# Weights decoded in pieces of twice the width, second half of x split three tiles at a time, w_out prepared two chunks at once

## The chip, the core and the metric

The kernel runs on one core of a Trainium2 chip, with its five engines: TensorE (PE, matrix products into PSUM banks), VectorE (DVE), ScalarE (ACT), GpSimd (POOL) and SyncE (SP), which here only issues DMAs. The metric is the time of one execution on the device in microseconds. Engines run their own instruction lists in order and meet through semaphores, so an instruction that waits also holds up everything behind it on its engine.

## The reference

Causal attention over 4 batches, 12 heads, 448 positions and head width 64, followed by two matrix products with a PReLU between them. The inputs q, k and v are float32. The two weights are float64 as they come.

```python
scores = scale * np.matmul(q, k.transpose(0, 1, 3, 2))
scores = np.where(mask, -1000000000.0, scores)      # causal
attn = np.exp(scores - max) / (sum + 1e-09)
x = np.matmul(attn, v)            # laid out as (1792, 768)
h = x @ w_in                      # (768, 2048)
g = np.maximum(h, 0.0) + alpha * np.minimum(h, 0.0)
out = g @ w_out                   # (2048, 768)
```

## The kernel before

**Products.** Both large products use a scheme of seven block products in place of eight (`STEPS`: P1, P5, P6, P2, P7, P3, P4). Its operands are blocks (A11, A12, A21, A22 of w_in, B11 to B22 of x or w_out) and sums of blocks (S1 to S4, T1 to T4). Each operand is split in a high part, which TensorE takes, and a low part, the rest; so every operand costs one cast on ACT (`a_cast`, `t_hi`, `w_cast`, `g_cast`) and one subtraction, called "lo" below, on DVE or POOL (`a_lo`, `t_lo`, `w_lo`, `g_lo`), beside the sums themselves (`a_sum`, `w_sum`, `g_sum`).

**Stages.** First comes attention, over 24 pairs of heads, in an order written out by hand (`ORDER`, `ROUNDS`). Into its iterations a table `EARLY` puts decoding work and splits of the first half of x (batches 0 and 1); the letters A, C, D, +, LD in it are the steps of a decode, h and l the cast and lo of one tile of x, S, cast and sub the sums and splits of w_in. Then comes the first product (line 395 on PE, `h_step`): 8 groups of 256 columns of w_in, each with 7 steps for each half of x (b = 0 and 1). Group 0 of the first half runs inside the end of attention. Groups 1 to 6 alternate b step by step; group 7 does b = 0 and then b = 1. The second product (line 1183, `o_step`) runs over four quarters Q of w_out's rows; each quarter has 7 tiles of 128 rows, taken in pairs that go on across the quarters' borders.

**Decoding.** A float64 weight arrives as two 32-bit words. `p_load` fetches a piece into a "raw" buffer (lines 273 and 278), ACT takes the magnitude of the high word (`p_abs`, line 290) and the scaled low word (`p_int`, 295), POOL or DVE clamps (`p_clamp`, 311 or 303), DVE shifts (`p_shift`, 303) and puts the sign back (`p_sign`, 319), POOL adds both words (`p_add`, 327). A piece has 384 values a partition: 32 pieces for w_in, 32 for w_out. A decoded piece of w_out is stored to DRAM (`wd`, line 331) and read back in the second product (line 1105). There are three raw buffers, two in the tile `dec` and one in `tf` that comes free after the split of T2 and T4; a raw buffer is given back after the sign.

**The order after attention** is made by a planner (`Plan`): jobs with an engine, a cost (`US`), dependencies, buffers that they take and give (`rooms`), and due times worked back from PE's list; each engine's order follows from it. It is fixed when the program is built. The handover from attention to the planned part holds the splits of the second half of x (`x2_jobs`): six operands of three tiles, 448 values a partition each, cast on ACT and subtracted on DVE or POOL (line 665). The first group's `h_plus` (line 409) on DVE, which adds a kept bank to another, stands between P6 and P7.

**w_out in the second product.** For each quarter and each of its two chunks u, `w_jobs` loads four blocks, makes four sums (line 1110) and seven splits (line 1121), all on DVE with 384 values a partition. The buffers of the quarter before come free step by step.

Of the kernel before, what the change touches and what calls it, by code (L numbers as in the profile page):

```python
# [21 lines left out]
CP = 112  # L22
QP = 128
WARM = 8
EARLY = {
# [25 lines left out]
    "abs": 0.56, "int": 0.56, "clamp": {"POOL": 0.53, "DVE": 0.48}, "shift": 0.48, "sign": 0.57, "add": 1.07, "cast": 0.53, "cast448": 0.57,  # L51
# [5 lines left out]
SHARED = {"sign", "sum", "lo", "lo448", "gsum", "glo"}  # L57
# [100 lines left out]
class Slots:  # L158
# [21 lines left out]
def kernel(  # L180
# [61 lines left out]
    def dec_of(i):  # L242
        return dec[:, 12 + i * NH : 12 + (i + 1) * NH]

    RAW = 2 * P + 2

    def rows_of(x, n):
        return x.bitcast(I32).rearrange("p (a n) -> p a n", n=n)[:, :, : 2 * P]  # L250
# [9 lines left out]
    raws, xs, ys, ss, wi = {}, {}, {}, {}, {}  # L260
# [7 lines left out]
    def p_load(key):  # L268
        kind, f, z = key
        t = raws[key] = rooms["raw"].take()  # L270
        if kind == "i":
            rows = w_in32[z * NH : (z + 1) * NH, 2 * f * P : 2 * (f + 1) * P]
# [1114 lines left out]
```

## Time and profile before

| | us |
|---|---|
| median of 3 runs | 618.72 (617.91 to 620.41) |
| the profiled execution | 618.8 |
| its span, first to last instruction | 617.0 |
| PE busy in the span | 582.4 (94%) |
| DVE busy | 506.6 (82%) |
| ACT busy | 403.0 (65%) |
| POOL busy | 314.4 (51%) |

The span lies 1.8 us below the execution's own time, and the profiled execution is 0.1 us from the median. PE is busy nearly throughout, so what can change the end is where PE waits, and at which clock it runs: the profile shows a granted clock of 1.0 (2.4 GHz) or 0.5 (1.2 GHz). A wait of PE has a releaser, the instruction that ended it, and the question at each is what stood in front of that releaser on its own engine.

### The profile page before, as it was taken

To read this page: it belongs to the slowest core of one execution; us is meant where nothing else is said; L and a number is where in the kernel's file an instruction comes from. 1 tells how busy PE (TensorE), PEld (TensorE's weight loads), DVE (VectorE), ACT (ScalarE), POOL (GpSimd) and SP (SyncE) were. 2 spreads that over 40 slices of the span, in tenths; PEclk is the share of its full clock that TensorE was granted. 3 is DMA by queue.
4 is the path that set the end of the run, shared out by engine and by line. 5 is a ranking of instruction groups with operands and counts; after the bars stand their busy time and mean duration, and the time that the engine had idled before them with its cause. 6 is when DMAs were issued, how large, how long until landed. Compare 5 with 4: busy or idle time off the path is not lost.

```text
span 617.0 us, 10794 instructions
## 1 busy us (share of the span) xinstructions
PE 582.4 (94%) x3300; PEld 502.0 (81%) x3300; DVE 506.6 (82%) x1118; ACT 403.0 (65%) x1002; POOL 314.4 (51%) x395
## 2 busy tenths in 40 slices
PE   8999999999975999999888989999999999988997
PEld 5666666667754989999777978999999999978997
DVE  5999888898479798988888795889788999887853
ACT  6999998888375665766566663778665755653521
POOL 7757687775354445554555431412635524581520
PEclk9999999999996999999899999999999999997999
DMA  6965636323053587867776737555242342221433
GB/s 166 215 130 159 171 89 185 107 75 118 17 159 123 169 252 236 292 208 248 238 236 210 253 141 240 159 163 163 81 133 70 93 132 82 82 70 55 166 90 116
DMA packets 100601, 93.98 MB, mean 152 GB/s; under 512 B 12736, under 2 KB 98848, under 8 KB 100544
## 3 DMA queue, kind: packets, MB, share of 16 engines
q1 hardware_dynamic: 99648, 91.66, 48.8%
q0 software_dynamic: 576, 1.18, 0.7%
q8 instruction: 26, 0.43, 0.3%
q10 hardware_dynamic: 320, 0.46, 0.2%
q14 instruction: 31, 0.25, 0.1%
HBM read 64.72 MB, written 28.54 MB: 151 GB/s over the span
## 4 chain that ended last, share of the span: by engine, by line
PE 77%; DVE 10%; DMA 6%; issue 3%; ACT 2%; SPq 1%; POOL 0%; ACTq 0%; DVEq 0%
PE bank L1183 27%; PE bank L395 26%; PE bank L602 7%; PE bank L582 7%; PE bank L525 6%; PE bank L517 4%; DMA dec<-in_moe_w_in_dram 2%; DVE x1h L1121 2%; DVE x2l L665 1%; DVE x1l L1161 1%; DVE dec L1110 1%; DMA tf<-gd 1%; DMA acc<-gd 1%; DMA dec<-wd 1%; SPq L1131 1%
## 5 line engine op out<-in xcount | busy, mean ns | idle before, releaser
L506 POOL TENSOR_SCALAR p<-p,rs 128x128 f32<-128x128 f32 (+3 forms) x164 | 83.8, 529 | 32.8 <-PE bank L525 11.1
L552 ACT ACTIVATE p<-bank,nm 128x256 f32<-128x256 f32 (+3 forms) x168 | 82.3, 505 | 14.8 <-DVE nm L537 9.1
L1183 PE MATMUL bank<-x1h,x1l 128*128 128x384 f32 x399 | 77.6, 336 | 2.4 <-DVE x1h L1121 1.9
L537 DVE CUSTOM_DVE_ANT_0 bank<-bank,mask 128x128 f32<-128x128 f32 (+3 forms) x168 | 71.1, 481 | 9.3 <-PE bank L525 5.4
L1183 PEld LDWEIGHTS bank<-x1h,x1l 128*128 128x128 f32 x399 | 70.0, 188 | 3.7 <-DVE x1h L1121 2.9
L1183 PE MATMUL bank<-x1h,gset 128*128 128x384 f32 x294 | 60.3, 343 | 0.9 <-DVE tf L1197 0.9
L419 ACT ACTIVATE tf<-bank 128x448 f32<-128x448 f32 x64 | 33.7, 541 | 38.1 <-PE bank L395 16.8
L1183 PEld LDWEIGHTS bank<-x1h,gset 128*128 128x128 f32 x294 | 53.2, 192 | 1.3 <-DVE tf L1197 1.3
L582 PEld LDWEIGHTS bank<-ident,p 128*128 128x128 f32 x384 | 43.3, 141 | 12.1 <-issue 8.1
L395 PE MATMUL bank<-x1h,wir 128*128 128x448 f32 x192 | 45.7, 371 | 5.6 <-DVE wir L377 5.1
L602 PEld LDWEIGHTS bank<-ptf,v 128*64 128x64 f32 x384 | 25.4, 136 | 30.8 <-issue 13.0
L395 PE MATMUL bank<-x2h,wir 128*128 128x448 f32 x174 | 43.2, 386 | 7.2 <-DVE bank L409 7.2
L423 DVE SCALAR_TENSOR_TENSOR tf<-tf,om,bank 128x448 f32<-128x448 f32 x64 | 41.8, 674 | 8.7 <-ACT tf L419 8.6
L582 PE MATMUL bank<-ident,p 128*128 128x128 f32 x384 | 47.5, 274 | 0.7 <-POOL p L506 0.5
L602 PE MATMUL bank<-ptf,v 128*64 128x448 f32 (+3 forms) x384 | 46.8, 386 | 0.0
L395 PEld LDWEIGHTS bank<-x2h,wir 128*128 128x128 f32 x174 | 35.0, 202 | 11.1 <-DVE bank L409 7.8
L395 PEld LDWEIGHTS bank<-x1h,wir 128*128 128x128 f32 x192 | 35.7, 188 | 10.1 <-DVE wir L377 6.2
L525 PE MATMUL bank<-kr,qr 64*128 64x128 f32 (+2 forms) x288 | 43.3, 404 | 0.0
L502 ACT ACTIVATE ptf<-bank 128x512 f32<-128x512 f32 (+1 forms) x71 | 38.0, 583 | 1.7 <-PE bank L582 1.7
L303 DVE TENSOR_SCALAR dec<-dec 128x384 int32<-128x384 int32 (+1 forms) x62 | 33.9, 546 | 5.8 <-POOL dec L311 3.1
L395 PE MATMUL bank<-x1h,wie 128*128 128x448 f32 x144 | 33.9, 368 | 4.4 <-DVE wie L377 4.4
L327 POOL TENSOR_TENSOR dec<-dec 128x384 int32<-128x384 int32 x26 | 28.6, 1102 | 17.9 <-DVE dec L319 10.1
(176 smaller groups left out, 1458.1 us busy)
## 6 DMA issues: line engine op xcount, KB each, us to landing
gd<-tf SPq DMA_DIRECT2D x64, 224.0 KB, 3.7
dec<-in_moe_w_in_dram SPq DMA_DIRECT2D x24, 384.0 KB, 3.9
dec<-in_moe_w_out_dram SPq DMA_DIRECT2D x22, 384.0 KB, 3.6
tf<-gd SPq DMA_DIRECT2D x28, 256.0 KB, 4.6
acc<-gd SPq DMA_DIRECT2D x28, 256.0 KB, 3.9
dec<-wd SPq DMA_DIRECT2D x28, 192.0 KB, 3.6
kr<-in_k_dram SPq DMA_DIRECT2D x44, 112.0 KB, 3.4
qr<-in_q_dram SPq DMA_DIRECT2D x47, 96.0 KB, 3.0
```

The costliest lines, as they stand in the source:

```text
L303: ts(out=out.bitcast(dtype), in0=x.bitcast(dtype), **how)
L395: nc.tensor.matmul(ps, w[:, u, k * P : (k + 1) * P], x[:, k], start=(st in ("P1", "P5") and i == 0), stop=(i == len(mms) - 1), skip_group_ ...
L419: nc.scalar.activation(t, bank_of(g, b, role), AF.Relu, scale=-1.0)
L423: stt(out=t, in0=t, scalar=om[:, f : f + 1], in1=bank_of(g, b, role), op0=ALU.mult, op1=ALU.add)
L502: eng.activation(out, x, AF.Copy, scale=side)
L506: eng.tensor_scalar(out=out, in0=x, scalar1=side, scalar2=1.0, op0=ALU.mult, op1=ALU.mult)
L525: nc.tensor.matmul(ps[:, o : o + lim], T["q", p][half(j), i * QP : (i + 1) * QP], T["k", p][half(j), :lim], start=(o == 0), stop=(n > 0 or ...
L537: nc.vector.tensor_tensor_reduce(out=t, in0=t, in1=masks[1] if i == NQ else masks[0][:, (NQ - 1 - i) * QP :], scale=-SCALE, scalar=MOST_F3 ...
L552: nc.scalar.activation(T["p", p, i][:, j, : t.shape[1]], t, AF.Exp, scale=-1.0, bias=T.pop(("nm", p, i, j)), accum_out=T["sm", p][:, z : z ...
L582: nc.tensor.transpose(ps[:, j - js[0], c], t[:, j, c * QP : (c + 1) * QP], T["ident"])
L602: nc.tensor.matmul(out[half(j), c * QP :], vs[b % 2][:, hp, c, j], x[:, c * QP : S], start=(c == 0), stop=(c == NQ),)
L1183: nc.tensor.matmul(ps, x, w, start=(st in ("P1", "P5")[: 1 if Q else 2] and i == 0), stop=(i == len(mms) - 1), skip_group_check=True,)
```

## The change

Four things change together.

1. A piece of the decode has 768 values a partition in place of 384: 16 pieces for w_in (both column halves of a group at once) and 16 for w_out (a whole chunk). The magnitude, clamp, shift and sign now work in place on the buffer `y`; the scaled low word is left in the raw buffer, which is therefore given back only after the add. There are two raw buffers of twice the size (one in `dec`, one in `tf`) in place of three, and four buffers y of twice the size in place of nine and three x. In attention three pieces are decoded early in place of five half-size ones.
2. The second half of x is cast and subtracted as a whole operand, 1344 values at once, except T1, which keeps its three tiles; all subtractions are on DVE, none on POOL. The loads of B21 and B22 are one DMA each.
3. The blocks of w_out are loaded, summed, cast and subtracted for both chunks of a quarter at once, 768 values, and sums T2, T3 and T4 overwrite one of their inputs.
4. The last three pieces of w_out (`LATE`) are loaded after the first product's last step and decoded in the first quarter of the second product, in space that later holds sums of output tiles 4 to 6.

The costs in `US` follow the new widths. The core of the diff:

```diff
+LATE = 3
...
-    25: "cast:A12 cast:S3 sub:A12 sub:S3", 26: "cast:S4 cast:A22 sub:S4 sub:A22",
+    25: "cast:A12 cast:S3 sub:A12 sub:S3", 26: "D:2 cast:S4 cast:A22 D:2 sub:S4 sub:A22 +:2:0 +:2:1 LD",
...
-        "raw": Slots([rows_of(dec[:, 3 * RAW * i : 3 * RAW * (i + 1)], RAW) for i in range(2)]),
-        "y": Slots([dec_of(i) for i in range(4, 8)]), "x": Slots([dec_of(i) for i in range(8, 10)]),
+        "raw": Slots([raw_of(dec_of(0, 4))]), "y": Slots([dec_of(i, 2) for i in (4, 6, 8)]),
...
+        low = parts_of(key)[0]
+        nc.scalar.activation(low.bitcast(I32), low, AF.Copy, scale=2.0**-29)
+
+    def p_clamp(key, eng=nc.gpsimd):
+        y = ys[key]
+        eng.tensor_scalar(out=y, in0=y, scalar1=MOST, scalar2=LEAST, op0=ALU.min, op1=ALU.max)
 
     def p_shift(key):
-        p_move(key, I32, scalar1=3, scalar2=0x3FFFFFF8, op0=ALU.logical_shift_left, op1=ALU.bitwise_and)
+        y = ys[key].bitcast(I32)
+        ts(out=y, in0=y, scalar1=3, scalar2=0x3FFFFFF8, op0=ALU.logical_shift_left, op1=ALU.bitwise_and)
...
+        y = line(ys[key]).bitcast(I32)
+        stt(out=y, in0=parts_of(key)[1], scalar=-0x40000000, in1=y, op0=ALU.bitwise_and, op1=ALU.bitwise_or)
+
+    def p_add(key, part=None):
+        y, low = line(ys[key]).bitcast(I32), parts_of(key)[0].bitcast(I32)
+        if part is not None:
+            y, low = y[:, :, part * P : part * P + P], low[:, :, part * P : part * P + P]
+        nc.gpsimd.tensor_tensor(out=y, in0=y, in1=low, op=ALU.add)
+        if part != 0:
+            rooms[room_of(key, "raw")].give(raws.pop(key))
...
+                for p in parts(nm):
+                    def hi(nm=nm, p=p):
+                        nc.scalar.activation(flat_of(XH[1][nm], nm, p), flat_of(x32(nm), nm, p), AF.Copy)
+
+                    def lo(nm=nm, p=p):
+                        x, h, l = (flat_of(t, nm, p) for t in (x32(nm), XH[1][nm], XL[1][nm]))
+                        nc.vector.tensor_tensor(out=l, in0=x, in1=h, op=ALU.subtract)
+
+                    n = S * (p[1] - p[0])
+                    job(("xh", nm, p), "ACT", f"cast{n}", hi, of)
+                    job(("x", 1, nm, p), "DVE", f"lo{n}", lo, [("xh", nm, p)])
...
+        at_end = T0 + (NG - 1) * PER
+        for j, key in enumerate(late_keys):
+            piece_jobs(key, before, at_end + 8.0 * j + 20.0, [("P", NG - 1, 1, "P4")])
+            before = key
...
+        def w_sum(Q, nm):
+            x, y = (at[Q, b] for b in W_SUMS[nm])
+            if nm == "T1":
+                t = at[Q, nm] = rooms["ws"].take()
+            else:
+                t = at[Q, nm] = at.pop((Q, {"T2": "T1", "T3": "B12", "T4": "B21"}[nm]))
+            nc.vector.tensor_tensor(out=t, in0=x, in1=y, op=ALU.subtract)
...
+            T1, T2 = (("wsum", Q, b) for b in ("T1", "T2"))
+            made = {
+                "B11": [B11], "T1": [B12, B11], "T2": [B22, T1, ("wlo", Q, "T1")], "B21": [B21], "T3": [B22, T1], "B22": [B22],
+                "T4": [T2, ("wlo", Q, "B21")],
...
+                        if t > 3:
+                            pl.wait_issue(pl.named[kind, q], [("store", key) for key in late_keys])
```

On DVE at the handover, before: from the last attention sum (L621) to the first group's two bank additions (L409) and the first activations (L423). The x2l rows are the lo parts of the second half of x, dec rows with L303 and L319 are shift and sign.

```order
L621 TENSOR_TENSOR tf<-bank_65,tf 128x448
L303 TENSOR_SCALAR dec<-dec 128x3x128
L319 SCALAR_TENSOR_TENSOR dec<-dec 128x384
L303 TENSOR_SCALAR dec<-dec 128x3x128
L319 SCALAR_TENSOR_TENSOR dec<-dec 128x384
L665 TENSOR_TENSOR x2l<-tf,x2h 128x448 x5
L303 TENSOR_SCALAR dec<-dec 128x3x128
L319 SCALAR_TENSOR_TENSOR dec<-dec 128x384
L665 TENSOR_TENSOR x2l<-x2l,x2h 128x448 x2
L665 TENSOR_TENSOR x2l<-tf,x2h 128x448 x3
L665 TENSOR_TENSOR x2l<-x2l,x2h 128x448 x2
L409 TENSOR_TENSOR bank_65<-bank_64,tf 128x448
```

On DVE at the same place now (L620, L961, L408, L307 and L311 are the same operations).

```order
L620 TENSOR_TENSOR tf<-bank_65,tf 128x448
L961 TENSOR_TENSOR x2l<-tf,x2h 128x448 x3
L961 TENSOR_TENSOR x2l<-tf,x2h 128x1344 x2
L961 TENSOR_TENSOR x2l<-x2l,x2h 128x1344
L408 TENSOR_TENSOR bank_65<-bank_64,tf 128x448
L961 TENSOR_TENSOR x2l<-x2l,x2h 128x1344
L307 TENSOR_SCALAR dec<-dec 128x768
L961 TENSOR_TENSOR x2l<-tf,x2h 128x1344
L311 SCALAR_TENSOR_TENSOR dec<-dec 128x768
L408 TENSOR_TENSOR bank_61<-bank_64,tf 128x448
```

The first bank addition stood behind twelve tiles of x and six steps of decode; now it stands behind T1's three tiles and three whole operands, and no decode step.

On SP in the middle of the first product, before: loads of pieces (L273, L278), stores of decoded w_out (L331) and of results (L429).

```order
L273 DMA dec<-in_moe_w_in_dram 128x3x256
L429 DMA gd_85<-tf 128x448 x2
L331 DMA wd<-tf 128x384
L278 DMA dec<-in_moe_w_out_dram 128x3x256
L429 DMA gd_85<-tf 128x448
L331 DMA wd<-tf 128x384
L273 DMA tf<-in_moe_w_in_dram 128x3x256
L278 DMA dec<-in_moe_w_out_dram 128x3x256
L273 DMA dec<-in_moe_w_in_dram 128x3x256
```

On SP in the middle of the first product now (L277 and L282 are the loads, L322 the stores of w_out, L428 of results).

```order
L277 DMA dec<-in_moe_w_in_dram 128x3x512
L428 DMA gd_85<-tf 128x448 x2
L322 DMA wd<-dec 128x768
L277 DMA tf<-in_moe_w_in_dram 128x3x512
L282 DMA dec<-in_moe_w_out_dram 128x1536
L428 DMA gd_85<-tf 128x448 x2
L282 DMA tf<-in_moe_w_out_dram 128x1536
L428 DMA gd_85<-tf 128x448 x3
L322 DMA wd<-dec 128x768
L277 DMA dec<-in_moe_w_in_dram 128x3x512
```

The loads now go to the two tiles in turn, one buffer each, where two of three went to `dec`; each brings twice as much.

On DVE where the fourth quarter begins, before: the rows between the additions of tiles 20 and 21 (L1197 from bank_67 and bank_68), of which tile 21 is the first of the fourth quarter; L1110 are sums and L1121 lo parts of its w_out.

```order
L1197 TENSOR_TENSOR bank_64<-bank_68,acc 128x384
L1110 TENSOR_TENSOR dec<-dec 128x384
L1197 TENSOR_TENSOR acc<-bank_65,acc 128x384 x2
L1197 TENSOR_TENSOR bank_63<-bank_67,tf 128x384
L1121 TENSOR_TENSOR x1h<-dec,x1h 128x384 x2
L1110 TENSOR_TENSOR dec<-dec 128x384
L1121 TENSOR_TENSOR x1l<-dec,x1l 128x384
L1121 TENSOR_TENSOR wie<-dec,wie 128x384
L1121 TENSOR_TENSOR x1h<-dec,x1h 128x384
L1110 TENSOR_TENSOR dec<-dec 128x384
L1110 TENSOR_TENSOR dec<-x1l,dec 128x384
L1197 TENSOR_TENSOR bank_61<-bank_68,acc 128x384
```

On DVE at the same place now (L1241 are the additions, L1165 the lo parts, L1206 a split of g).

```order
L1241 TENSOR_TENSOR bank_64<-bank_68,acc 128x384
L1165 TENSOR_TENSOR x1h<-dec,x1h 128x2x384
L1206 TENSOR_TENSOR x1l<-acc,x1l 128x512
L1241 TENSOR_TENSOR acc<-bank_65,acc 128x384
L1241 TENSOR_TENSOR bank_63<-bank_67,tf 128x384
L1241 TENSOR_TENSOR acc<-bank_65,acc 128x384
L1241 TENSOR_TENSOR bank_61<-bank_68,acc 128x384
```

Between tile 21's two bank additions stood eight instructions on w_out; now there is one, and four of the quarter's seven operands are split before tile 20 begins.

## Rows read from the trace of the kernel before

**Rows 1.** The page: its head.
```profile
span 617.0 us, 10794 instructions
```

**Rows 2.** Busy time by stretch: stretch, us, busy us of each engine (instructions), granted clock, DMA.
```profile
164.40:201.00 36.60, 25.65 (x110) 20.25 (x110) 26.50 (x35) 20.39 (x45) 17.28 (x17) 0.86 0.36 119
201.00:395.20 194.20, 183.83 (x884) 166.23 (x883) 165.28 (x302) 121.40 (x254) 89.76 (x97) 0.99 0.68 222
395.20:614.00 218.80, 210.33 (x1177) 207.17 (x1175) 176.33 (x274) 122.09 (x250) 89.99 (x62) 0.98 0.37 110
```

**Rows 3.** Waits of PE: engine, line, releaser, us in total, times, longest.
```profile
PE bank L395 <- DVE bank L409: 7.7, 3, 6.8
PE bank L395 <- DVE wir L377: 5.1, 3, 2.3
PE bank L1183 <- DVE wie L1121: 4.5, 2, 4.3
PE bank L395 <- DVE wie L377: 4.4, 2, 2.5
```

**Rows 4.** Timeline at the handover, of PE, DVE, ACT: start, us, instructions, idle before.
```profile
174.50 2.92 ACT L502 ACTIVATE x2h<-tf 128x448 fp32r<-128x448 f32 x6 [0.65 <-DMA xd_B<-low_B]
...
175.58 5.19 DVE L665 TENSOR_TENSOR x2l<-tf,x2h 128x448 fp32r<-128x448 f32 x5
...
192.22 0.62 DVE L409 TENSOR_TENSOR bank<-bank,tf 128x448 f32<-128x448 f32 x1
...
192.89 2.61 PE L395 MATMUL bank<-x2h,wir 128*128 128x448 f32 x6 [6.80 <-DVE bank L409]
...
200.91 1.39 PE L395 MATMUL bank<-x1h,wie 128*128 128x448 f32 x6
...
204.59 1.39 PE L395 MATMUL bank<-x1h,wir 128*128 128x448 f32 x6
```

**Rows 5.** Loads of pieces, 203 to 356 us: first, last, and grouped with landing time.
```profile
203.35 0.38 SPq L278 DMA_DIRECT2D dec<-in_moe_w_out_dram  x1
...
355.07 0.38 SPq L278 DMA_DIRECT2D dec<-in_moe_w_out_dram  x1
...
dec<-in_moe_w_out_dram SPq DMA_DIRECT2D x21, 384.0 KB, 3.6
dec<-in_moe_w_in_dram SPq DMA_DIRECT2D x14, 384.0 KB, 3.7
tf<-in_moe_w_out_dram SPq DMA_DIRECT2D x10, 384.0 KB, 4.0
...
tf<-in_moe_w_in_dram SPq DMA_DIRECT2D x7, 384.0 KB, 4.4
```

**Rows 6.** DMA issues of the whole run: KB each, median us to landing.
```profile
b<-xd_B SPq DMA_DIRECT2D x1, 672.0 KB, 4.9
```

**Rows 7.** Groups by shape: count, busy us, mean ns; L303's row: shortest, median, longest ns.
```profile
L377 DVE TENSOR_TENSOR wie<-dec,wie 128x384 fp32r<-128x384 f32 x16 | 8.8, 553 | 0.3 <-ACT wie L374 0.3
L1161 DVE TENSOR_TENSOR x1l<-dec,x1l 128x512 fp32r<-128x512 f32 x11 | 7.5, 682 | 0.2 <-ACT x1l L1157 0.2
L303 DVE TENSOR_SCALAR tf<-tf x21: 352/690/1169, 204.6 to 356.0; 128x384 int32<-128x384 int32 x18, 128x384 f32<-128x384 f32 x3
L327 POOL TENSOR_TENSOR tf<-tf,dec 128x384 int32<-128x384 int32 x20 | 20.3, 1017 | 21.8 <-DVE dec L319 15.6 <-ACT wir L374 2.6 <-ACT dec L290 2.1
L374 ACT ACTIVATE wir<-dec 128x384 fp32r<-128x384 f32 x25 | 12.8, 524 | 3.8 <-DVE dec L345 2.9 <-POOL dec L327 0.8
L1157 ACT ACTIVATE x1l<-dec 128x512 fp32r<-128x512 f32 x19 | 11.9, 627 | 8.7 <-DVE dec L1151 8.1 <-POOL dec L1151 0.4
```

**Rows 8.** Timeline where the fourth quarter begins, of DVE and PE.
```profile
551.99 2.53 DVE L1121 TENSOR_TENSOR x1h<-dec,x1h 128x384 fp32r<-128x384 f32 x2
554.45 1.61 DVE L1110 TENSOR_TENSOR dec<-dec 128x384 f32<-128x384 f32 x1
...
558.12 1.01 PE L1183 MATMUL bank<-wie,x1l 128*128 128x384 f32 x2 [4.30 <-DVE wie L1121]
```

More of the change, by code (lines that the diff above doesn't have):

```diff
@@ L50 @@
 US = {
-    "abs": 0.56, "int": 0.56, "clamp": {"POOL": 0.53, "DVE": 0.48}, "shift": 0.48, "sign": 0.57, "add": 1.07, "cast": 0.53, "cast448": 0.57,
+    "abs": 0.82, "int": 0.82, "clamp": {"POOL": 0.83, "DVE": 0.56}, "shift": 0.56, "sign": 0.97, "add": 2.02, "cast": 0.53,
+    "cast448": 0.57, "cast1344": 1.2, "lo1344": 1.55, "wsum": 0.95, "wcast": 0.8, "wlo": 0.95,
     "sum": {"DVE": 0.57, "POOL": 1.15}, "lo": {"DVE": 0.56, "POOL": 1.15}, "lo448": {"DVE": 0.63, "POOL": 1.25},
@@ L55 @@
 }
-SHARED = {"sign", "sum", "lo", "lo448", "gsum", "glo"}
+SHARED = {"clamp", "shift", "sign", "sum", "lo", "lo448", "lo1344", "gsum", "glo", "wsum", "wlo"}
 LOAD, STORE = 4.0, 3.0
@@ L268, in p_load @@
     def p_load(key):
[L269 to L272, printed above, removed]
+        t = raws[key] = rooms[room_of(key, "raw")].take()
+        if key[0] == "i":
+            _, g, z = key
+            rows = w_in32[z * NH : (z + 1) * NH, 4 * g * P : 4 * (g + 1) * P]
             nc.sync.dma_start(
@@ L323, in p_sign @@
-        rooms["raw"].give(raws.pop(key))
-    def p_add(key):
-        y, x = ys[key].bitcast(I32), xs[key].bitcast(I32)
-        nc.gpsimd.tensor_tensor(out=y, in0=y, in1=x, op=ALU.add)
-        rooms["x"].give(xs.pop(key))
+        y = line(ys[key]).bitcast(I32)
[7 more added lines that the diff above has]
+            rooms[room_of(key, "raw")].give(raws.pop(key))
@@ L966, in x_of @@
                 return []
-            return [("x", 1, nm, k) for k in range(KW)]
+            return [] if nm == "B11" else [("x", 1, nm, p) for p in parts(nm)]
         def step_job(g, b, st):
@@ L1187, in o_step @@
             if t == NTT - 1:
-                for u in range(2):
-                    rooms["w"].give(wo.pop((Q, u, bn)).rearrange("p u n -> p (u n)"))
+                rooms["w"].give(wo.pop((Q, bn)).rearrange("p u h n -> p (u h n)"))
             if q % 2:
@@ new lines, in w_jobs @@
+            for c, z in ((0, 0), (0, 1), (1, 1), (1, 0)):
+                job(
+                    ("wl", Q, f"B{c + 1}{z + 1}"), "SP", "issue", lambda c=c, z=z: w_load(Q, c, z),
+                    dec_end + [("store", ("o", 4 * Q + c + 2 * u)) for u in range(2)], "wf", lag=LOAD, behind=list(wl_last),
+                )
+                wl_last[:] = [("wl", Q, f"B{c + 1}{z + 1}")]
+            B11, B12, B22, B21 = (("wl", Q, b) for b in ("B11", "B12", "B22", "B21"))
+            T1, T2 = (("wsum", Q, b) for b in ("T1", "T2"))
@@ new lines, in w_jobs, with give @@
+            made = {
+                "B11": [B11], "T1": [B12, B11], "T2": [B22, T1, ("wlo", Q, "T1")], "B21": [B21], "T3": [B22, T1], "B22": [B22],
+                "T4": [T2, ("wlo", Q, "B21")],
+            }
+            gives = {"B11": "B11", "T1": "B11", "T2": "B22", "T3": "B22", "T4": "T2"}
+            def give(nm):
+                n = W_READS.get(nm, 1)
+                return [("ws" if nm == "T2" else "wf", Q, nm, n)]
+            for st in STEPS:
+                nm = STEP[st][1]
+                of = made[nm]
+                if nm[0] == "T":
+                    job(("wsum", Q, nm), "DVE", "wsum", lambda nm=nm: w_sum(Q, nm), of, "ws" if nm == "T1" else "", give(gives[nm]))
+                    of = [("wsum", Q, nm)]
+                job(("wcast", Q, nm), "ACT", "wcast", lambda nm=nm: w_cast(Q, nm), of, "w")
+                job(
+                    ("wlo", Q, nm), "DVE", "wlo", lambda nm=nm: w_lo(Q, nm), [("wcast", Q, nm)],
+                    give=[] if nm in ("T1", "B21") else give(nm),
+                )
```

294 lines of the change are left out of this document (133 added, 161 removed), and 6 rows, old and new, of the table EARLY.

## The prediction

> **What bounds the kernel now.** I read the page's head [rows 1], then busy time by stretch [rows 2], then the waits of PE with their releasers [rows 3], then the timelines around the two longest of them [rows 4, 8], and last the loads and the groups by shape [rows 5 to 7]. The stretches show PE busy 184 of 194 us in the first product and 210 of 219 in the second; only the handover is loose, 25.7 of 36.6, with a granted clock of 0.86 [rows 2]. So the end is PE's own work plus three sets of waits. One is the wait of 6.8 us on L409 at the handover, followed by matmuls at the half clock: 2.61 us for six at 192.89, where six take 1.39 at 200.91 [rows 3, 4]. The second is the first product's waits for weights, 5.1 + 4.4 = 9.5 us on L377. The third is 4.5 us on L1121, nearly all in one wait of 4.3 where the fourth quarter begins [rows 3, 8].
>
> **Handover: -10.7 us.** L409 starts at 192.22 because twelve tiles of x (L665) and two decode steps stand before it on DVE from 175.58 on; five of those tiles took 5.19 us, 1.04 each [rows 4]. Now three tiles and three whole operands stand there. An operation with two inputs takes 0.62 at 448 values (L409's row), 0.553 at 384 and 0.682 at 512, so about 1.0 ns a value plus little: 1344 values are 0.68 + 832 x 1.04 ns = 1.55 us [rows 4, 7]. DVE then needs 3 x 0.62 + 3 x 1.55 = 6.5 us: from 175.58 to 182.1. ACT can feed this: its casts start at 174.50, three tiles at 0.49 and then wide ones at about 1.27 (0.627 + 832 x 0.8 ns) [rows 4, 7], three of them by 179.8. So the bank addition runs near 182.2 and P7 starts at 182.8, not 192.89. What is late next: the remaining whole operands (about 1.3 us of cast and 1.55 of lo each) against a step of 1.84 us (204.59 - 200.91 is two steps). P3 starts at 184.7, and P4 waits some 1.4 us for its operand, which stands behind a cast, a sign and another lo: 187.9 to 189.8. With 0.4 for the split of A11, group 1 starts at 190.2 where it started at 200.91: **-10.7**. That takes the clock as full, as no wait is longer than 1.5 us. Bounds: DVE as slow as the 1.04 us tiles throughout (1.7 times) costs 4.5; no wait at P4 gains 1.4.
>
> **First product: -2.9 us.** Here the buffers decide. The 52 loads of pieces go from 203.35 to 355.07 [rows 5], one every 2.975 us, with three raw buffers: a buffer turns over in 8.9 us. The new turn C holds twice the values and, new, the add. Load: 384 KB land in 3.6 to 4.4, 672 KB in 4.9 [rows 5, 6], so 768 KB in about 5.2, +1.2. Magnitude on ACT, 0.524 to 0.83: +0.3. Clamp +0.3. Sign 0.55 to 0.95: +0.4. Shift: the rows of L303 run from 352 to 1169 ns with a median of 690 [rows 7]; at the shortest row's speed 768 values take 0.55 to 0.70, so I take no change. The add on POOL, 1.017 at 384 [rows 7], 2.03 at 768, plus 0.3 to 0.4 until POOL takes it: +2.4. C = 8.9 + 4.6 = **13.5 us**. Each of two buffers then gives 768 values per 13.5 us where three gave 384 per 8.9: 114 a us, before 129. That is slower, and yet enough until near the end, because three of the 16 pieces of w_out are taken out of this stretch. The buffer in `dec` is free from about 189.4 (its piece of attention is decoded before the split ends). The twelfth load into it from there is the last piece of w_in, decoded at 189.4 + 12 x 13.5 = 351.4. PE wants it, with a sum and split before, about 0.6 before group 7. A group is 14 steps of 1.84, 25.8 us, so group 7 starts at 190.2 + 6 x 25.8 = 345.0, and the piece is 7.0 us late. The loss is 7.0 plus one fall of the clock, about 1.5; now it is 9.5 plus 1.9 (a granted clock of 0.99 over 194.2 us [rows 2]). 8.5 - 11.4 = **-2.9**. Break-even is C = 12.9, and each 0.1 us of C above it is 1.2 us of time: this is the most sensitive term. DVE itself gets lighter: 22 half-size decode operations a group (at 0.55, 12.1 us) become 8 (0.55 to 0.95, 6.0 us), and it was busy 165.3 of 194.2 [rows 2], so it isn't what delays the pieces.
>
> **From the first product to the second: +2.5 us.** As the last pieces come late, the loads of the first quarter of w_out start later against PE. Nothing of before shows that; it lies between 0 and one landing of such a load, 4 to 5 us [rows 5, 6]. I take the middle.
>
> **Fourth quarter: -6 us.** Eight instructions on w_out stand on DVE between the additions of tile 21; L1121 is behind several of them and ends the 4.30 us wait [rows 8]. Now one is left, and four of seven operands are split earlier, in the pair before. Removed: 4.5 of waits, and the half clock behind them. The granted clock is 0.98 over 218.8 us [rows 2], 4.4 us lost in all, of which I give 2.5 to this wait. About 1 us remains for a split that is met late. -4.5 - 2.5 + 1 = **-6**; bounds -8.5 and -3.
>
> **Late pieces and wide splits: +1 us.** Three pieces decode in the first quarter: per piece 0.7 + 0.95 us on DVE, about 3 us on POOL, 0.83 twice on ACT, in a stretch where DVE is busy 176 of 219 and POOL 90 [rows 2]. They hide in that room; what doesn't hide is that ACT's eviction of tile 4 must wait for a store. Bounds 0 and one landing, 4; I take 1. **Attention: 0.** It decodes one half-size piece more, 0.69 + 0.55 us on DVE over 24 iterations; bounds 0 and 1.2.
>
> Sum against the profiled execution, 0.1 from the median: 618.8 - 10.7 - 2.9 + 2.5 - 6 + 1 = 602.7. I say **602**; the bounds of the terms, taken as independent (root of the sum of their squares, with 0.3 us either way in C, 3.6 of time), put it some 5 below and 8 above: 597 to 610.
>
> **The page that speaks against it.** The row shows that a shift took from 352 to 1169 ns at one shape [rows 7], and that x's tiles took 1.04 where another operation of that width took 0.62 [rows 4]; POOL was at work in that stretch for 17.3 of 36.6 us [rows 2]. The Trainium skill, "SBUF — State Buffer", section "Who interferes with whom", says that VectorE and GpSimd contend for one shared pair of ports, held for a whole instruction, so that the loser is fully blocked. By that, POOL's total hold is unchanged (half as many adds, twice as long), but one collision costs up to 2.03 instead of 1.02. That is the slower rival below.
>
> **Rivals.**
> *The turn is shorter.* If the larger load lands in 4.9 [rows 6] and the wait for POOL is nil, C is 12.9 or less and no piece is late: the first product's loss goes, 602.7 - 8.5 = **594**. For it: landing times grow less than bytes, and only two loads are in flight. Against: all stages double in width, and nothing in the chain overlaps with itself.
> *The handover waits for a reload.* B21 comes by one DMA of 672 KB where thirds came before; if a whole operand's cast stands in front of it, PE waits one landing, 4.9 us [rows 6]: 602.7 + 4.9 = **608**. Against: the casts start at 174.50 with the same DMA wait as before [rows 4].
> *Long adds hold up the decode.* Each buffer's shift and sign meet the other buffer's add (2.03 us) and wait for about half of it, 1.0 each: C = 15.5. The last piece is then ready at 189.4 + 186 = 375.4, 31 us late, and 24 us are lost against the sum: **626**, slower than before. It decides from C = 15.1, where the total gain is below zero by 0.5%. For it: the shifts of 1.17. Against: the median of 0.69, and that POOL is busy only 90 of 194 us in the first product [rows 2].
> *It comes out even.* C between 14.6 and 15.1 gives back all gains elsewhere: **619**.
>
> **How the numbers follow.** 0.5%, 3.1 us, is about what a measurement of this kernel can tell from no change: 615.6 to 621.8. Forecast 0.46, the shorter turn 0.20, the reload 0.09: faster 0.75. Even 0.09. Slower 0.16, nearly all of it the long adds. The range goes from 590 (the short turn with the better ends of the handover and the fourth quarter) to 618, which leaves out the slower cases and a few hundredths below.
>
> **What would show it.** Right: group 1's first step near 190, P7's wait on L408 below 2 us with no half clock after it; loads into the same buffer 13.5 us apart; waits on L376 of 6 to 8 us in all, most of it before group 7; no wait over 1 us when the fourth quarter begins. Wrong: loads 15 us apart and waits on L376 of 20 us and more; a wait for a load of B21; waits of PE for output tile 4 or for the first quarter's w_out above 5 us; iterations of attention that are longer.

## The result: 593.6 us, where the first product never waits for weights

The changed kernel takes 593.56 us (median of 4 runs, 592.09 to 595.25) beside 618.32 for the kernel before: a ratio of 0.9602, 95% interval 0.9553 to 0.9650. That is inside the range given (590 to 618), on the forecast side, and 8 us below the likeliest value, 602. It is the time of the rival "the turn is shorter" (594).

The profiled execution took 592.1 us. The page's head and its row of PE, which answer to [rows 1]:

```profile
span 590.3 us, 10250 instructions
PE 573.7 (97%) x3300; PEld 496.8 (84%) x3300; DVE 470.2 (80%) x1000; ACT 389.0 (66%) x900; POOL 290.1 (49%) x334
```

Busy time by stretch (us, then PE, PEld, DVE, ACT, POOL, granted clock, DMA), to be read beside [rows 2]: the handover up to group 1, the first product, the second.

```profile
164.40:190.50 26.10, 22.55 (x108) 17.98 (x109) 17.21 (x20) 13.77 (x21) 6.58 (x6) 1.00 0.39 126
190.50:376.80 186.30, 182.56 (x883) 166.51 (x883) 140.31 (x226) 112.43 (x196) 77.62 (x54) 0.99 0.66 221
376.80:586.60 209.80, 206.89 (x1177) 204.88 (x1176) 174.73 (x252) 122.60 (x233) 88.51 (x56) 1.00 0.43 132
```

The handover is 10.5 us shorter and at the full clock, where it was granted 0.86. DVE does 25 us less in the first product (140.3 for 165.3). The waits of PE, which answer to [rows 3]:

```profile
PE bank L394 <- DVE bank L408: 3.8, 3, 2.3
PE bank L1228 <- ACT bank L1337: 1.7, 1, 1.7
PE bank L394 <- ACT bank L401: 1.6, 1, 1.6
PE bank L394 <- DVE tf L422: 1.4, 1, 1.4
...
PE bank L1228 <- DVE wo L1165: 0.8, 2, 0.5
```

There is no row for L376 at all, which was L377: the 9.5 us of waits for weights are gone. The bank additions cost 3.8 us where they cost 7.7, and L1165, which was L1121, 0.8 here (and 0.4 in a row not shown) where it cost 4.5 (and 1.9 in a row not shown). Three waits are new or longer: L1337 on ACT, the fork L401 on ACT (0.5 before), and L422 on DVE.

The handover, from the timeline of PE and DVE (start, us, instructions, idle before), beside [rows 4]:

```profile
175.33 1.70 DVE L961 TENSOR_TENSOR x2l<-tf,x2h 128x448 fp32r<-128x448 f32 x3 [4.45 <-ACT x2h L957]
177.49 3.03 DVE L961 TENSOR_TENSOR x2l<-tf,x2h 128x1344 fp32r<-128x1344 f32 x2 [0.46 <-ACT x2h L957]
180.96 1.56 DVE L961 TENSOR_TENSOR x2l<-x2l,x2h 128x1344 fp32r<-128x1344 f32 x1 [0.45 <-ACT x2h L957]
182.43 0.63 DVE L408 TENSOR_TENSOR bank<-bank,tf 128x448 f32<-128x448 f32 x1
183.31 1.57 PE L394 MATMUL bank<-x2h,wir 128*128 128x448 f32 x6
190.52 1.51 PE L394 MATMUL bank<-x1h,wie 128*128 128x448 f32 x6
```

The bank addition starts at 182.43 and PE goes on at 183.31 without a wait; group 1 starts at 190.52, where it started at 200.91. The wait of 1.4 us on L422 falls just behind that point, at 194.05.

The loads of pieces into the buffer in `dec` after attention, the first, the second and the last of twelve, beside [rows 5]:

```profile
190.08 0.40 SPq L282 DMA_DIRECT2D dec<-in_moe_w_out_dram  x1
...
205.58 0.41 SPq L282 DMA_DIRECT2D dec<-in_moe_w_out_dram  x1
...
327.91 0.38 SPq L277 DMA_DIRECT2D dec<-in_moe_w_in_dram  x1
```

Inside the first product a turn of this buffer is (327.91 - 205.58) / 10 = 12.2 us. The forecast counted from the load at the end of the handover: its twelve loads, with a first turn of 15.5, give (327.91 - 190.08) / 11 = 12.5. It had 13.5, and 12.9 as the point below which nothing is late.

Where the first product ends, the timeline of POOL, DVE and PE shows the wait that is left:

```profile
366.55 1.71 POOL L1196 TENSOR_TENSOR tf<-tf 128x512 f32<-128x512 f32 x1
...
367.05 2.02 DVE L1154 TENSOR_TENSOR dec<-dec 128x768 f32<-128x768 f32 x1
368.99 0.62 DVE L408 TENSOR_TENSOR bank<-bank,tf 128x448 f32<-128x448 f32 x1
...
369.67 1.50 PE L394 MATMUL bank<-x2h,wie 128*128 128x448 f32 x6 [2.33 <-DVE bank L408]
...
372.05 2.44 PE L394 MATMUL bank<-x2h,wir 128*128 128x448 f32 x6
```

A sum of w_out stands before the last bank addition on DVE. Beside a POOL operation it takes 2.02 us; at 525.12 (below) the same shape takes 0.95. PE waits 2.33, and six matmuls then take 2.44 in place of 1.39: from 372.0 to 374.3 the granted clock is 0.50.

Where the fourth quarter begins, DVE and POOL (beside [rows 8]):

```profile
525.12 0.95 DVE L1154 TENSOR_TENSOR dec<-dec 128x768 f32<-128x768 f32 x1
...
534.00 3.28 PE L1228 MATMUL bank<-x1h,x1l 128*128 128x384 f32 x18
...
534.67 2.02 DVE L1165 TENSOR_TENSOR x1l<-dec,x1l 128x768 fp32r<-128x768 f32 x1
535.83 2.01 POOL L1196 TENSOR_TENSOR acc<-acc 128x512 f32<-128x512 f32 x1
536.61 2.04 DVE L1165 TENSOR_TENSOR wie<-dec,wie 128x768 fp32r<-128x768 f32 x1
```

Splits of w_out are stretched here too, to 2.02 and 2.04 us, but PE has operands to work on and does not wait.

### The profile page after: what moved, and what is told of

Read it like the earlier page. It is cut to its first block, busy times and chain, and to the rows that moved or that the text cites. A ratio compares the mean times of both kernels' runs of the same rounds, so it can differ in the third digit from the quotient of the medians.

```text
span 590.3 us, 10250 instructions
## 1 busy us (share of the span) xinstructions
PE 573.7 (97%) x3300; PEld 496.8 (84%) x3300; DVE 470.2 (80%) x1000; ACT 389.0 (66%) x900; POOL 290.1 (49%) x334
## 5 line engine op out<-in xcount | busy, mean ns | idle before, releaser
L1228 PE MATMUL bank<-x1h,x1l 128*128 128x384 f32 x456 | 83.9, 335 | 0.4 <-DVE x1h L1165 0.4
L1228 PEld LDWEIGHTS bank<-x1h,x1l 128*128 128x128 f32 x456 | 79.7, 188 | 0.7 <-DVE x1h L1165 0.7
L422 DVE SCALAR_TENSOR_TENSOR tf<-tf,om,bank 128x448 f32<-128x448 f32 x64 | 41.5, 674 | 15.5 <-ACT tf L418 15.5
L581 PEld LDWEIGHTS bank<-ident,p 128*128 128x128 f32 x384 | 43.2, 141 | 12.5 <-issue 8.6
L394 PE MATMUL bank<-x1h,wir 128*128 128x448 f32 x186 | 43.2, 368 | 0.5 <-DVE bank L408 0.5
L1228 PE MATMUL bank<-x1h,gset 128*128 128x384 f32 x216 | 41.0, 338 | 1.7 <-ACT bank L1337 1.7
L524 PE MATMUL bank<-kr,qr 64*128 64x384 f32 (+2 forms) x288 | 42.3, 399 | 0.0
L1228 PEld LDWEIGHTS bank<-x1h,gset 128*128 128x128 f32 x216 | 37.9, 188 | 2.2 <-ACT bank L1337 2.0
L394 PE MATMUL bank<-x2h,wir 128*128 128x448 f32 x156 | 37.5, 377 | 0.9 <-DVE bank L408 0.9
L317 POOL TENSOR_TENSOR dec<-dec,tf 128x768 int32<-128x768 int32 x13 | 25.6, 1968 | 26.0 <-ACT tf L418 9.8
L551 ACT ACTIVATION_READ_ACCUMULATOR p<-bank,nm 128x1 f32 x168 | 35.2, 210 | 0.0
L394 PE MATMUL bank<-x2h,wie 128*128 128x448 f32 x132 | 30.9, 369 | 3.9 <-DVE bank L408 2.3
```

The lines of the kernel that those rows point to most:

```text
L317: nc.gpsimd.tensor_tensor(out=y, in0=y, in1=low, op=ALU.add)
L394: nc.tensor.matmul(ps, w[:, u, k * P : (k + 1) * P], x[:, k], start=(st in ("P1", "P5") and i == 0), stop=(i == len(mms) - 1), skip_group_ ...
L422: stt(out=t, in0=t, scalar=om[:, f : f + 1], in1=bank_of(g, b, role), op0=ALU.mult, op1=ALU.add)
L524: nc.tensor.matmul(ps[:, o : o + lim], T["q", p][half(j), i * QP : (i + 1) * QP], T["k", p][half(j), :lim], start=(o == 0), stop=(n > 0 or ...
L551: nc.scalar.activation(T["p", p, i][:, j, : t.shape[1]], t, AF.Exp, scale=-1.0, bias=T.pop(("nm", p, i, j)), accum_out=T["sm", p][:, z : z ...
L581: nc.tensor.transpose(ps[:, j - js[0], c], t[:, j, c * QP : (c + 1) * QP], T["ident"])
```

## The experiments

Times are compared with the kernel before, run on the same chip (its medians on the three chips used were 618.15, 619.07 and 618.98). The changed kernel was run again on the third of them only: 593.09 us. For runs on the other two, the ratio is to be compared with its 0.9602 (0.9553 to 0.9650).

### What made the handover shorter

The first run undoes the width of x's operations alone.

```diff
-            return [(k, k + 1) for k in range(KW)] if nm == "T1" else [(0, KW)]
+            return [(k, k + 1) for k in range(KW)]
```

> Undoes the width alone at the handover: the second half of x is cast and subtracted in tiles of 448 again, still on VectorE only. With narrow tiles the planned order puts thirteen tiles and two decode steps before the first bank addition. Theory (VectorE's queue ahead of that addition is the price, each tile 0.63 us with no GpSimd work beside it): 13 x 0.63 + 0.56 + 0.95 = 9.7 us in place of 6.5, so the addition runs near 185.6 in place of 182.4, group 1 starts 3 to 5 us later (half clock behind a wait of 3), time 597 to 599. Rival (the width decides, one operation costs much more than 0.63 us in such a row): the wait of 6.8 us comes back, group 1 near 200, time 603.

Measured: 598.0 us (ratio 0.9674, 0.9635 to 0.9714). The bank addition on DVE, and PE behind it:

```profile
185.16 0.62 DVE L408 TENSOR_TENSOR bank<-bank,tf 128x448 f32<-128x448 f32 x1
...
185.83 1.49 PE L394 MATMUL bank<-x2h,wir 128*128 128x448 f32 x6 [2.58 <-DVE bank L408]
```

The addition is at 185.16, the wait 2.58: the theory's numbers. Only group 1 starts earlier than it said, at 192.49, 2.0 us behind the changed kernel and 8.4 ahead of the kernel before; a wait of 3.1 on L422 comes behind it. A tile without POOL beside it costs 0.55 to 0.62 here, so narrow tiles are not dear by themselves. What costs is what the planner then puts in front of the addition: one tile more and two decode steps. Then the question is why the kernel before waited 6.8. Its DVE tiles took 1.04 while POOL also subtracted. The next run lets POOL take tiles again (`"DVE|POOL"` for `"DVE"`, tiles of 448).

> As the tiles of 448, but the subtractions may also go to GpSimd, as before the change. Theory that GpSimd's share stretched the tiles (1.04 us each in the kernel before against 0.62): the stretch comes back, the bank addition runs near 190, group 1 near 199, time 601 to 604. Rival (the queue's length alone): some tiles leave VectorE, the addition is no later than with all tiles on VectorE, time 596 to 599.

Measured: 594.16 us (0.9617, 0.9567 to 0.9667), and a wait of 3.04 on the addition, at 185.21. Neither the theory's time came nor the rival's, and the run does not tell between them: planned anew, all of the first twelve tiles went to DVE and POOL took its first at 183.49 (2.80 us long). But group 1 starts at 193.05, 2.5 us behind the changed kernel, and the time can't be told from the changed kernel's. So what the width of x's operations is worth in the whole time depends on the rest of the order and is not shown by these runs. The next run puts the middle tile of every operand on POOL for good; the core of its edit:

```diff
-                    job(("x", 1, nm, p), "DVE", f"lo{n}", lo, [("xh", nm, p)])
+                    job(("x", 1, nm, p), "DVE" if p[0] != 1 else "POOL", f"lo{n}", lambda lo=lo, p=p: lo(nc.vector if p[0] != 1 else nc.gpsimd), [("xh", nm, p)])
```

> The second half of x in tiles of 448, and the middle tile of each operand is put on GpSimd for good; in the last run with a choice the planner left nearly all on VectorE, so the tiles met no GpSimd work. Theory (GpSimd's subtractions stretch VectorE's): tiles of 1.0 us and more on VectorE, 1.5 to 2.8 on GpSimd; the first bank addition waits for them, near 187 to 190, time 598 to 602. Rival (fewer tiles on VectorE help): ten of them before the addition at 0.55 us, addition at 184 or earlier, time 593 to 595.

Measured: 596.76 us (0.9641, 0.9605 to 0.9676). DVE and POOL between the fourth operand and the addition, with the step of PE that waited:

```profile
185.28 2.71 DVE L961 TENSOR_TENSOR x2l<-tf,x2h 128x448 fp32r<-128x448 f32 x2
186.01 1.50 POOL L961 TENSOR_TENSOR x2l<-tf,x2h 128x448 fp32r<-128x448 f32 x1
...
187.92 1.48 DVE L307 TENSOR_SCALAR dec<-dec 128x768 int32<-128x768 int32 x1
...
189.86 0.62 DVE L408 TENSOR_TENSOR bank<-bank,tf 128x448 f32<-128x448 f32 x1
...
190.53 2.61 PE L394 MATMUL bank<-x2h,wir 128*128 128x448 f32 x6 [4.07 <-DVE bank L408]
```

Two tiles take 2.71 us beside POOL's, a shift 1.48 in place of 0.56, and PE waits 4.07 although DVE has four tiles fewer to do. (In this profile the first subtraction came 3.6 us later than in the changed kernel's, so starts are compared from it: addition after 10.9 us here, 9.4 with all tiles on DVE, 7.1 with whole operands, 16.6 before.) That bears the theory out in the place. In the whole time it is not shown: 3 to 4 us up, less than the theory said, with an interval that overlaps the changed kernel's. And no run brings the 16.6 of the kernel before back, where POOL also did three adds in that stretch.

### What sets the first product

> LATE = 0: the last three pieces of w_out are decoded inside the first product again. Theory (two raw buffers with a turn of 12.4 us have only about 2 us to spare): the last piece of w_in is then the fourteenth load into its buffer, ready at 187 + 14 x 12.4 = 361 where it is wanted at 344.5: 16 us of waits for weights (L376) and one fall of the clock, time 608 to 612. Rival (lighter VectorE is what removed the waits, the buffers have room): below 3 us, 592 to 597.

Edit: `LATE = 3` becomes `LATE = 0`. Measured: 600.95 us (0.9721, 0.9683 to 0.9759). Its waits of PE:

```profile
PE bank L394 <- ACT wie L372: 7.9, 2, 6.3
```

The waits for weights are back (9.9 us in all, with 1.2 on L376 and 0.8 on the cast of `wir`), 6.3 of them before the second step of the last group. The direction is the theory's, and the rival (room in the buffers) is out; the time is 7 to 11 us less than it said. The waits are 9.9 and not 16, and though the first output tile comes 13 us later (389.70 in place of 376.83), the second product then runs in 205.7 us in place of 209.8, without a wait in the list: no pieces are decoded in it any more.

A second run lengthens the turn: each clamp is done twice, except on the first two groups' pieces of w_in.

```diff
-        eng.tensor_scalar(out=y, in0=y, scalar1=MOST, scalar2=LEAST, op0=ALU.min, op1=ALU.max)
+        for _ in range(2 if key[0] == "o" or key[1] > 1 else 1):
+            eng.tensor_scalar(out=y, in0=y, scalar1=MOST, scalar2=LEAST, op0=ALU.min, op1=ALU.max)
```

> The clamp runs twice on every piece loaded in the planned part (the second changes no value): 0.84 us more in each turn of a raw buffer, which GpSimd has room for. Theory (break-even of the turn near 12.6, each 0.1 us beyond it 1.2 us): turn 13.2 to 13.4, last piece of w_in 7 to 10 us late, time 601 to 606. Rival (the turn has slack, since the chain waits elsewhere): the loads stay 12.2 to 12.5 apart, time 593 to 595.

Measured: 598.59 us (0.9678, 0.9629 to 0.9727). Its first and last load into `dec`:

```profile
206.15 0.41 SPq L282 DMA_DIRECT2D dec<-in_moe_w_out_dram  x1
...
333.76 0.38 SPq L277 DMA_DIRECT2D dec<-in_moe_w_in_dram  x1
```

The turn grew by 0.5, to 12.8, not by 0.84, and the time by 5 us: 2.7 us of waits for weights came back (one of 2.2), and 0.7 on a bank addition. So the turn does decide. By the forecast's own count, from the load at 190.43, it is (333.76 - 190.43) / 11 = 13.0, just above the break-even of 12.9, which this run does not contradict.

### Why the turn was 12.2 and not 13.5

The diff has a line that neither my account of the change nor my sum took in: the planner's list `SHARED`, the operations on DVE that it never places beside one on POOL, was given the clamp, the shift, and the new names of x's and w_out's operations. (It keeps them apart in its plan; in the trace they still meet at times, as the stretched sum above does.)

```diff
-SHARED = {"sign", "sum", "lo", "lo448", "gsum", "glo"}
+SHARED = {"clamp", "shift", "sign", "sum", "lo", "lo448", "lo1344", "gsum", "glo", "wsum", "wlo"}
```

One run puts back the old line whole.

> The planner's list of operations that it keeps apart from GpSimd's goes back to the one of before (clamp, shift, wsum, wlo and lo1344 out of it); nothing else changes. Theory (widths and the late pieces made the gain): within 2 us of the changed kernel, 592 to 596. Rival (planning around GpSimd made a part of it): operations on VectorE are stretched beside GpSimd's, waits of 3 us and more come back in the second product, 597 or more.

Measured: 630.23 us, slower than the kernel before: 1.0184, 1.0169 to 1.0199. Its longest waits of PE:

```profile
PE bank L394 <- DVE bank L408: 9.0, 6, 3.8
...
PE bank L1228 <- DVE bank L1241: 5.1, 4, 2.5
```

and its lo parts of w_out on DVE (busy us, mean ns):

```profile
L1165 DVE TENSOR_TENSOR x1h<-dec,x1h 128x768 fp32r<-128x768 f32 x16 | 24.1, 1533 | 0.8 <-ACT x1h L1161 0.8
```

The rival holds, by far more than it said: 1.53 us a split in place of 1.23 in the changed kernel (0.95 undisturbed). The first output tile comes at 398.66, 21.8 us later, and the second product takes 226.9 us, 17.1 more. But the old line also takes the sums and splits of w_out out of the list, which before the change were in it as "sum" and "lo", and those of whole operands of x ("lo448" before). So this run is not the kernel before with wider operations: it lacks a protection that the kernel before had. The next run takes out only what is truly new, the clamp and the shift.

> The changed kernel with clamp and shift alone taken out of the planner's list of operations kept apart from GpSimd's; sums and lo parts of w_out stay in it, as they were before the change under other names. Theory (the list's two new entries keep the shift and the clamp from meeting in a turn of the raw buffer): the turn goes from 12.2 to 13.4 or more, shifts beside GpSimd work of 0.8 us and more in place of 0.56, waits for weights of 3 to 8 us come back, 598 to 606. Rival (the 36 us lost with the whole list came from the sums and lo parts of w_out): turn 12.5 or less, 592 to 596.

Measured: 599.65 us (0.9694, 0.9648 to 0.9740), 6.6 above the changed kernel on the same chip. Its loads into `dec`, its shifts (shortest, median, longest ns), and DVE's busy time in 25 shifts; then the last two for the changed kernel:

```profile
207.30 0.42 SPq L282 DMA_DIRECT2D dec<-in_moe_w_out_dram  x1
...
340.97 0.38 SPq L277 DMA_DIRECT2D dec<-in_moe_w_in_dram  x1
...
L307 DVE TENSOR_SCALAR dec<-dec x22: 546/560/2223, 32.6 to 349.7; 128x768 int32<-128x768 int32 x22
...
190.00:358.00 168.00, 24.99 (x25) 0.99 0.65 215
```

```profile
L307 DVE TENSOR_SCALAR dec<-dec x21: 547/557/691, 31.4 to 343.4; 128x768 int32<-128x768 int32 x21
...
190.00:345.00 155.00, 14.83 (x25) 1.00 0.68 229
```

The turn is 13.4 us (13.6 by the forecast's count), near the 13.5 that the prediction worked out, and the time is near its 602. The median shift is the same, but single shifts take up to 2.22 us, where the longest in `dec` in the changed kernel is 0.69 and in `tf` 1.32; 25 shifts take 25.0 us in place of 14.8. The theory holds, except that the waits came as much on bank additions and forks (5.1 on L408 for 3.8, 4.0 on L401 for 1.6) as on L376 (2.6): work that waits on DVE and ACT beside the decode is late as well. From group 1 to the first output tile it takes 195.4 us in place of 186.3, of which the second product gives back 2.4 (207.3 for 209.8). The other 30 us between this run and the one before belong to the new names; that is a difference of two runs, and was not tried by itself.

Does the list alone help the kernel before?

```diff
-SHARED = {"sign", "sum", "lo", "lo448", "gsum", "glo"}
+SHARED = {"clamp", "shift", "sign", "sum", "lo", "lo448", "gsum", "glo"}
```

> The kernel before with nothing but clamp and shift added to that list. Theory (a part of the gain is this list's and not the widths'): shifts of 0.35 us (alone) for those of 0.7, the waits on L377 of 9.5 us shrink by 3 to 6, 611 to 615. Rival (with narrow pieces VectorE has no room to keep out of GpSimd's way; it pays only with the wide ones): 617 to 622.

Measured: 634.46 us, 2.5% slower than before (1.0253, 1.0204 to 1.0302). Both expectations fail. Its waits, the row of its clamps on POOL in `dec`, and last the shifts and clamps on DVE in `dec` in the kernel before:

```profile
PE bank L395 <- DVE wie L377: 9.4, 4, 3.6
...
PE bank L395 <- ACT wir L374: 6.4, 2, 4.0
PE bank L395 <- DVE wir L377: 3.8, 4, 2.0
...
L311 POOL TENSOR_SCALAR dec<-dec x46: 500/508/874, 37.8 to 375.2; 128x384 f32<-128x384 f32 x46
...
L303 DVE TENSOR_SCALAR dec<-dec x62: 537/546/557, 39.4 to 361.2; 128x384 int32<-128x384 int32 x46, 128x384 f32<-128x384 f32 x16
```

The entries had little to win here. The narrow shifts in `dec` were not stretched before either, as the last row shows (0.56 us at most); only the 18 in `tf` get shorter (a median of 0.42 us for 0.69), and the clamps a little (0.87 at most in `dec` for 1.41). What they cost shows in the loads: the 52 from 206.13 on end at 370.19 in place of 355.07. All 64 clamps are on POOL now, where DVE took 19 of them before, and every shift must find a gap of POOL in the plan; which of the two slows the decode was not separated. Waits for weights double, from 9.5 us to these 19.6.

So four runs on one chip can be set side by side (us):

| | the list without clamp and shift | with them |
|---|---|---|
| pieces and operands as before | 618.98 | 634.46 |
| the changed kernel's | 599.65 | 593.09 |

The widths and late pieces gain 19 us without the two entries and 41 with them; the two entries gain 6.6 in the wide kernel and lose 15 in the narrow one. That they help only with the wide pieces is the main thing these runs show.

### What the wide operations on w_out are worth

The sums, casts and lo parts of w_out are made for one chunk at a time, each job planned by itself; in short:

```diff
-                job(("wcast", Q, nm), "ACT", "wcast", lambda nm=nm: w_cast(Q, nm), of, "w")
...
+                for u in range(2):
...
+                    job(
+                        ("wcast", Q, nm, u), "ACT", "cast", lambda nm=nm, u=u: w_cast(Q, nm, u), of, "" if u else "w",
+                        behind=[("wcast", Q, nm, 0)] if u else (),
+                    )
```

> Sums, casts and lo parts of w_out are made for one chunk at a time again (384 values, twice as many instructions, planned one by one); loads and buffers as in the changed kernel. Theory that the wide operations opened the fourth quarter: eight instructions stand between two additions again, a wait of 2 to 4 us on L1165 where the fourth quarter begins and a fall of the clock, 597 to 599. Rival (the earlier order, from loads and buffers for both chunks at once, did it): no wait above 1 us there, below 2 us in all, 593 to 595.5.

Measured: 604.28 us (0.9762, 0.9746 to 0.9779). Its waits:

```profile
PE bank L394 <- DVE bank L408: 5.8, 3, 3.9
...
PE bank L1231 <- DVE bank L1244: 1.6, 2, 1.4
```

Neither expectation is right. The width is worth some 10 us, more than the theory said, but not at its place: the fourth quarter begins with a wait of 1.4, behind five and not eight instructions on w_out, and the rest lies at the end of the first product (3.9) and in the first two quarters (6.3 in all, on DVE and ACT). The second product takes 217.4 us in place of 209.8. So the forecast's "eight instructions between two additions" was one place of several. DVE is busy 179.8 us in that product, 5 more than in the changed kernel; that this load is the cause all through the stage is likely and not shown, as the whole order was planned anew.

### The waits that are left

The wait of 2.33 us on the last bank addition can be met by order: the sum T2 of w_out and one lo part are planned behind it.

```diff
+        for late in (("wsum", 0, "T2"), ("glo", 0, "S2")):
+            pl.wait_issue(pl.named[late], [("Z", NG - 1, 1)])
```

> In the planned order the first quarter's sum T2 of w_out (L1154) and the lo part of the sum S2 of g may start only behind the last bank addition Z of the first product (L408), which in the changed kernel stands behind them: the sum took 2.02 us there, beside a GpSimd operation, in place of 0.95, and TensorE waited 2.33 us, with two steps at the half clock after it. Theory (VectorE's queue, and that one stretched sum, is what PE waits for): the wait falls below 1 us, no half clock, 590 to 591.5 in place of 593.6. Rival (what is put behind is missed in the first steps of the second product instead): new waits of 2 us or more on L1165 or L1206 between 376 and 400 us, time 593 to 595.

Measured: 591.76 us (0.9553, 0.9534 to 0.9572). PE's wait there falls to 1.20 with no half clock, and the first output tile starts at 374.84 in place of 376.83. Then part of it comes back:

```profile
PE bank L1228 <- DVE wo L1165: 2.7, 2, 1.6
```

L1165 costs 2.7 where it cost 0.8. Both theories are half right. The interval overlaps that of the changed kernel (0.9599, 0.9556 to 0.9641, in its second measurement below), so it is not shown to be better.

The wait of 1.7 on L1337 stays. It is the price of the late pieces. In the changed kernel ACT stands 2.94 us for the second late piece's load, and the fork behind it holds PE:

```profile
394.27 0.90 ACT L295 ACTIVATE tf<-tf 128x768 f32<-128x768 f32 x1 [2.94 <-DMA tf<-in_moe_w_out_dram]
...
396.88 0.85 ACT L1337 ACTIVATE bank<-bank 128x384 f32<-128x384 f32 x2
```

In one more run, on top of the last one, that piece is planned behind the forks of tiles 2 and 3.

```diff
+        for q in (2, 3):
+            pl.wait_issue(pl.named["abs", late_keys[1]], [("ofork", q)])
```

> The version with the last bank addition put first, and with the second late piece's ACT work (L295) planned behind the forks of output tiles 2 and 3, since ACT waited 2.9 us for that piece's load and the fork (L1337) behind it held PE for 1.7 us. Theory (ACT's queue is the price of the late pieces): the wait on L1337 falls below 0.7 us, 589 to 590.5. Rival (the late pieces then hold the first quarter's later tiles): a new wait of 1 us or more, 591 to 593.

> The changed kernel once more, beside the version with both moves on one chip: 592 to 595, and the two apart by 2 to 4 us if both moves work, by less than 1 if not.

Measured on one chip: 594.05 us (0.9596, 0.9552 to 0.9640) against 593.09 (0.9599, 0.9556 to 0.9641) for the changed kernel. No gain: ACT now stands before the same fork for another load, that of g, and PE waits 5.3 us on the fork where it waited 1.7. Both expected times of the version are missed.

```profile
395.24 1.67 ACT L1202 ACTIVATE x1l<-tf 128x512 fp32r<-128x512 f32 x3 [7.26 <-DMA tf<-gd]
...
397.34 2.93 PE L1228 MATMUL bank<-x1h,gset 128*128 128x384 f32 x8 [5.26 <-ACT bank L1337]
```

The piece was in front, but not the only thing in front. No version tried is shown to beat the changed kernel.

## Why the prediction held, and which of its terms did not

| term | forecast | measured, from the profiled executions |
|---|---|---|
| handover, to group 1's first step | -10.7 | -10.4 (200.91 to 190.52) |
| first product, and its end | -2.9 + 2.5 | -7.8 (194.1 to 186.3 us up to the first output tile) |
| second product | -6 + 1 | -8.8 (218.6 to 209.8) |
| tail | 0 | +0.3 |
| sum | -16.1 | -26.7 |

**Handover: right, in size and place.** The addition was put at 182.2 and came at 182.43; P7 at 182.8, came at 183.31; P4's wait at 1.4, was 0.9; group 1 at 190.2, came at 190.52. Of the 10.4 us, 0.6 came from an attention that ended earlier. Not in the sum were two waits, 1.6 us on the fork L401 ahead of the addition, and 1.4 on L422 behind group 1's start, which counts in the next row. Of the reasons, the runs with tiles show two, in the place and not in the time: tiles put more in front of the addition (7.1 to 9.4 us after the first subtraction), and POOL beside them stretches them (10.9). The rest of the 16.6 before was not brought back by any run.

**First product: the mechanism was right and the size wrong.** The term that failed is the turn C: 13.5, where twelve loads measure 12.5 (12.2 without the first turn). Its parts, as means over the 23 pieces loaded from 201 to 334 us, and in brackets over the 52 before: load's issue to the magnitude 5.4 (4.7), so 0.7 longer for 1.2; the waits from the magnitude through clamp and shift to the sign 1.1 in all (1.7), where the sum carried the 1.7 over; the sign 0.95 and the shift 0.56, as forecast; the add 2.0 with 0.2 before it, for 2.4. So it was in part the rival "the turn is shorter", whose conditions were a landing of 4.9 (the groups' medians are 4.3 to 5.3) and no wait for POOL (0.2). The other part is the list, a line of the diff that the sum left out: with clamp and shift out of it, the turn is 13.4 and the time 599.7. But that this turn meets the forecast's 13.5 is luck. There the waits between the steps are 0.8, shorter and not longer; what grows is the shift (a mean of 1.0 for 0.56), which the sum took as undisturbed, the time to the magnitude (5.7) and the wait before the add (0.5). Why the waits between the steps fell from 1.7 no run separates.

The sensitivity was about right. From a turn of 12.9 on the formula gives 1.2 us for each 0.1 and 1.5 for the clock: 10 us at the 13.6 of the run without the two entries, 3 at the 13.0 of the doubled clamp. Measured from group 1 to the first output tile, they are 9.1 and 5.2 longer than the changed kernel, which lies below the break-even and has no wait for weights.

**First product to the second: the size was near, the cause wrong.** PE waited for no load of w_out. It waited 2.33 us for the last bank addition, behind a stretched sum, and lost 1.7 to the clock (granted 0.86 over the 12.4 us up to the first output tile).

**Second product: right in sign, too small.** Every wait at the fourth quarter went, and the clock's loss with it (granted 0.98 to 1.00). The run with single chunks shows that the gain is not only there. **Late pieces:** forecast +1, measured a wait of 1.7 on ACT, where the forecast had it, though for a load and not for a store. They pay for this: with `LATE` at 0, 7 us are lost.

**The slower rival** (long adds hold up the decode, 626) did not come. A part of its mechanism did where the list lacked clamp and shift: shifts stood behind adds, and the turn was 13.4, not the rival's 15.5. That the run with the whole old list came near its time, at 630 us, is luck: its turn is (345.15 - 189.55) / 11 = 14.1, and 17 of its 37 us are lost in the second product, of which the rival does not speak. The Trainium skill, "SBUF — State Buffer", section "Who interferes with whom", says that of a VectorE and a GpSimd operation that meet on their shared ports the loser is fully blocked. The trace agrees: 2.02 us for a sum of 0.95 that meets a POOL operation, 2.22 for a shift of 0.56. The rival's chance, 0.16, hung on the order of the operations, which could be read in the list beforehand.

## What to carry to other kernels

Where a planner sets the order, its tables are part of the change: in a line that says which operations must not overlap, two new entries were worth 7 us, and leaving out the renamed ones as well cost 37. Try widths and such rules together and apart: here the two entries alone made the kernel 2.5% slower, the widths and late pieces without them 3% faster, and all together 4%. When a chain through several engines is widened, do not carry its waits over from the old trace; ask what stands in front of each link in the new order. And measure a mean the way the forecast counts it: without its first turn the same buffer looks 0.3 us faster, and a break-even that held seems to fail.

## What was not expected of the hardware

Sums, splits and shifts on DVE that start while an operation runs on POOL take about the rest of that one longer. The split at 536.61 meets a POOL operation with 1.23 us to go and takes 1.09 more than its 0.95. A bank addition at 538.58, beside a POOL operation from 537.80 to 539.84, took its usual 0.55. In all, a sum of 768 values took 0.95 or 2.02 us, a shift 0.56 or up to 2.22, and a subtraction of 448 on POOL 1.16 or 2.80. But the narrow shifts in `dec`, in the kernel before, took 0.54 to 0.56 throughout; why those were never stretched no run here shows. For the decode in wide pieces, in which the two alternate, planning them apart was worth 1.1 us in a turn of 12.2; in narrow ones it cost.
